# Values' product on array tiles of 64 rows by 32 columns instead of 64 by 64

## The chip, the cores and the metric

The kernel runs on one core of one Trainium2 chip. The time is that of the device for one execution, in microseconds (us); a smaller one is better. Before the change the median of three runs is 661.97 us, and they lie from 660.65 to 662.07. The engines are TensorE (PE in the profile, with its weight loads as PEld), VectorE (DVE), ScalarE (ACT), GpSimd (POOL) and SyncE (SP, which issues transfers).

## The reference

Eight batches go through windowed attention, then through a gated convolution, then through a gated block that mixes positions:

```python
scores = scale * np.matmul(q, k.transpose(0, 1, 3, 2))     # (8, 8, 576, 64) each
# heads 0-3: the last 32 positions; heads 4-7: every 4th of the last 128
scores = np.where(masks[None, :, :, :], scores, -1000000000.0)
scores = scores - np.max(scores, axis=-1, keepdims=True)
attn = np.exp(scores)
attn = attn / (np.sum(attn, axis=-1, keepdims=True) + 1e-09)
x = np.matmul(attn, v)                                      # heads side by side: (8, 576, 512)
gate = sigmoid(causal_conv5(x, conv_w))
x = gate * (x @ w_val) @ w_out
h = np.maximum(x @ w_in, 0.0)
u, v = h[..., :512], h[..., 512:]
v_n = (v - mean(v)) / np.sqrt(var(v) + 1e-06)
v_s = np.einsum('ts,bsd->btd', w_spatial, v_n) + b_spatial
out = (u * v_s) @ w_out2
```

## The kernel before

All work lies on one core, batch after batch. Each batch has an attention part, four pairs of heads (p = 0 to 3; the two heads of a pair lie in partitions 0 to 63 and 64 to 127), and a part of large products (`val`, `v`, `u`, `sp`, `out`) with 128 by 128 tiles of the array. The attention of a later batch is put in between the large products of an earlier one. The order is written out by hand: two tables, `EARLY` for the start and `EVERY` with a period for the rest, give each piece of work a due time; a queue sorted by these times emits the instructions, and each engine runs its own in that order.

For a pair of batches 2 to 7 (the third to the eighth) the attention does this. `a_scores` multiplies queries with keys: 36 products, each with 64 rows (the values of a head), 32 weight columns (32 queries) and 64 moving columns (64 keys), so tiles of 64 by 32 of the array. Mask, maximum, exponential and sum follow on other engines, then a transpose on VectorE and small transfers put the weights of the attention into `pt_later`. `a_pv` clears the border of its output tile and goes on in `pv_later`, which the change touches: the values' product. Its weights are the values `u` (64 keys by 64 value columns of one head), its moving operand is `pt_later` (64 keys by 96 queries). Five blocks `j` of 128 keys, two heads `h` and two halves `r` of a block (the last block has one half) give 18 products, written to the accumulator `o`: the head's 64 partitions, and a bank of the accumulator for each half `r`. Each is a product in 32-bit floats. After it, ScalarE and VectorE add the two halves into the input of the convolution (`xt`, or `tt` for the second four heads).

TensorE takes instructions in the written order. In most places of batches 3 on, the values' product of one pair is followed directly by the scores of a later pair (`qk_t`, `s_ps`), and then by the large products again. All instructions are emitted by one helper (line 635), so the rows of the profile have that one line, and groups are told apart by their tiles: `o_ps` is the accumulator of the values' product, `s_ps` that of the scores.

Of the kernel before, what the change touches and what calls it, by code (L numbers as in the profile page):

```python
# [25 lines left out]
QB = 32  # L26
# [647 lines left out]
def attention_gated_mlp_kernel(  # L674
# [29 lines left out]
    pt_later = pt.rearrange("p a b c q -> p (a b c q)")[:, 0:2 * NK * 96]  # L704
    pt_later = pt_later.rearrange("p (h j i q) -> p h j i q", h=2, j=NK, i=3)
# [26 lines left out]
    def matmul(o, a, r, start, stop):  # L732

        ten.matmul(o, a, r, start=start, stop=stop)
# [189 lines left out]
    def a_pv(b, p):  # L924
        if b == 0:
            xt = act.tile([128, 4 + S], F32, tag=f"xh{p}", name="xt")
            xh[b, p] = xt[:, 4:]
        else:
            xt = rot.tile([128, XW], F32, tag="xt", name="xt")
        gps.memset(xt[:, 0:4], 0.0)  # L930
        yield
        u = vv_t.pop((b, p))
        o = ps_o.tile([128, 1024], F32, tag="o", name="o_ps")
        if b >= 2:
            yield from pv_later(b, p, u, o, xt)
            return
        for j in range(NJ):
            c = 512 * (j // 3) + 96 * (j % 3)
            for h in range(2):
                r = slice(64 * h, 64 * h + 64)  # L940
                matmul(o[r, c:c + 96], u[:, j, r], pt[:, :, h, j], True, True)
        o = o.rearrange("p (a c) -> p a c", a=2)[:, :, 0:HS]
        if p < 2 and (b or p == 0):
            o_t[b, p] = o
        yield
        x_t[b, p] = xt
        if p < 2:
            sca.copy(out=xt[:, 4:4 + S].rearrange("p (a c) -> p a c", a=2), in_=o)
        else:
            sca.copy(  # L950
                out=xt[:, 4:4 + S].rearrange("p (i a r) -> p a r i", a=2, r=2),
                in_=o.rearrange("p a (r i) -> p a r i", r=2),
            )

    def pv_later(b, p, u, o, xt):


        for j in range(NK):
            for h in range(2):
                d = slice(64 * h, 64 * h + 64)  # L960
                for r in range(2 if j < NK - 1 else 1):
                    k = slice(64 * r, 64 * r + 64)
                    w = pt_later[k, h, j].rearrange("p i q -> p (i q)")
                    matmul(o[d, 512 * r + 96 * j:512 * r + 96 * j + 96], u[k, j, d], w, True, True)
        yield
        y = xt[:, 4:]
        if p >= 2:
            tt[b, p] = y = act.tile([128, S + 64], F32, tag=f"tt{p}", name="tt")
        gap = y[:, 96:96 + 512].rearrange("p (j c) -> p j c", c=128)[:, :, 0:QB]
        gps.memset(gap, 0.0)  # L970
        yield
        sca.copy(
            out=y[:, 0:640].rearrange("p (j c) -> p j c", c=128)[:, :, 0:96],
            in_=o[:, 0:480].rearrange("p (j c) -> p j c", c=96),
        )
        yield
        later = y[:, 64:64 + 512].rearrange("p (j c) -> p j c", c=128)[:, :, 0:96]
        vec.tensor_tensor(
            out=later, in0=o[:, 512:896].rearrange("p (j c) -> p j c", c=96), in1=later, op=ALU.add
        )  # L980
        if p >= 2:
            yield
            sca.copy(
                out=xt[:, 4:4 + S].rearrange("p (i g) -> p g i", g=4), in_=y[:, 0:S].rearrange("p (g i) -> p g i", g=4)
            )
        x_t[b, p] = xt
# [484 lines left out]
```

## Time and profile before

| | |
|---|---|
| median of 3 runs | 661.97 us (660.65 to 662.07) |
| span of the profiled execution | 659.2 us |
| TensorE busy | 638.3 us, 97% |
| VectorE busy | 455.7 us, 69% |
| GpSimd busy | 309.1 us, 47% |
| ScalarE busy | 305.2 us, 46% |
| granted TensorE clock, mean | 0.999 |

The span goes from the first to the last instruction that the profiler recorded; the timed runs hold something more than the span. Busy time is the union of an engine's instructions, and a product in 32-bit floats stands in it as two matmuls and two weight loads. A matmul's duration counts from its start to the end of what it writes, so matmuls that follow each other overlap in the records. A time line merges neighbours of one kind in a row with a count; asked for a short window, it shows the instructions that are in flight in the window, with the start of the earliest.

### The profile page before, as it was taken

The page shows a single profiled execution, that of the slowest core. Times are in us where ns is not written, and L with a number is a line of the kernel's source. Part 1 is how long each engine was busy: PE and PEld are TensorE (multiplying, and loading weights), DVE is VectorE, ACT ScalarE, POOL GpSimd, SP SyncE. Part 2 cuts the span into 40 slices and gives each one's busy share as a digit, 9 for nine tenths or more (in the row PEclk, how much of TensorE's full clock was granted, in tenths as well). Part 3 has the DMA queues.
Part 4 walks back from the last instruction along what each step waited for, and adds up shares of the span by engine and source line. Part 5 has one row for each costly group of instructions (what it writes and reads, how often), then busy time and mean ns, then how long its engine had stood idle before and what let it go on. Part 6 is the DMA issues. An engine that isn't in the chain of part 4 may idle for free.

```text
span 659.2 us, 17770 instructions
## 1 busy us (share of the span) xinstructions
PE 638.3 (97%) x7248; PEld 586.2 (89%) x7248; DVE 455.7 (69%) x789; ACT 305.2 (46%) x702; POOL 309.1 (47%) x378
## 2 busy tenths in 40 slices
PE   2899999999999999999999999999999999999998
PEld 2547789999899989999899989999899989999997
DVE  4999688997686677767666688767676688533410
ACT  4887666444443434344443435443443434442422
POOL 1114996746543374436634464426634464524430
PEclk9999999999999999999999999999999999999999
DMA  8981333353133332343123433343133411120002
GB/s 326 407 296 38 113 106 126 87 153 71 39 108 81 87 78 78 79 133 96 34 76 96 117 74 77 80 131 99 31 75 97 119 40 41 19 75 1 1 1 72
DMA packets 85605, 63.58 MB, mean 96 GB/s; under 512 B 64530, under 2 KB 74642, under 8 KB 85012
## 3 DMA queue, kind: packets, MB, share of 16 engines
q1 hardware_dynamic: 76308, 53.01, 28.5%
q10 hardware_dynamic: 9216, 9.44, 4.2%
q8 instruction: 57, 0.93, 0.6%
q14 instruction: 24, 0.20, 0.1%
HBM read 44.92 MB, written 9.44 MB: 82 GB/s over the span
## 4 chain that ended last, share of the span: by engine, by line
PE 82%; DVE 9%; DMA 3%; ACT 3%; POOL 2%; issue 1%; SPq 0%; DVEq 0%; POOLq 0%
PE sp_ps L635 17%; PE out_ps L635 15%; PE u_ps L635 14%; PE v_ps L635 14%; PE val_ps L635 14%; PE o_ps L635 4%; PE s_ps L635 3%; DVE tt L635 3%; DMA raw<-in_w_in 2%; DMA raw<-in_w_mid_t 1%; DVE wo_f L635 1%; DVE wiu_f L635 1%; POOL wsp_l L635 1%; ACT pt L635 1%; DVE v_t L635 1%
## 5 line engine op out<-in xcount | busy, mean ns | idle before, releaser
L635 DVE SCALAR_TENSOR_TENSOR tt<-xt,cw,tt 128x576 f32<-128x576 f32 x116 | 118.6, 1028 | 1.2
L635 PE MATMUL sp_ps<-wsp_h,vh 128*128 128x288 f32 x320 | 93.7, 297 | 0.0
L635 POOL TENSOR_TENSOR gl<-tt,gh 128x288 fp32r<-128x288 f32 x64 | 61.1, 963 | 49.6 <-ACT gh L635 45.9
L635 POOL TENSOR_TENSOR g2l<-ru,g2h 128x288 fp32r<-128x288 f32 x64 | 55.7, 877 | 53.8 <-ACT g2h L635 53.6
L635 PE MATMUL u_ps<-gh,w_h 128*128 128x288 f32 x256 | 76.3, 298 | 0.0
L635 PE MATMUL out_ps<-g2h,wout_h 128*128 128x288 f32 x256 | 76.2, 298 | 0.0
L635 PE MATMUL out_ps<-g2h,wout_l 128*128 128x288 f32 x256 | 75.4, 295 | 0.1
L635 PE MATMUL out_ps<-g2l,wout_h 128*128 128x288 f32 x256 | 75.4, 295 | 0.0
L635 PE MATMUL sp_ps<-wsp_l,vh 128*128 128x288 f32 x256 | 75.4, 294 | 0.0
L635 PE MATMUL u_ps<-gh,w_l 128*128 128x288 f32 x256 | 75.4, 294 | 0.0
L635 PE MATMUL u_ps<-gl,w_h 128*128 128x288 f32 x256 | 75.4, 294 | 0.0
L635 PE MATMUL sp_ps<-wsp_h,vl 128*128 128x288 f32 x256 | 75.4, 294 | 0.0
L635 PE MATMUL val_ps<-xh,wval_h 128*128 128x288 f32 x224 | 67.0, 299 | 0.0
L635 PE MATMUL val_ps<-xl,wval_h 128*128 128x288 f32 x224 | 66.2, 296 | 0.0
L635 PE MATMUL val_ps<-xh,wval_l 128*128 128x288 f32 x224 | 66.1, 295 | 0.0
L635 POOL TENSOR_TENSOR xl<-xt,xh 128x576 fp32r<-128x576 f32 x28 | 42.6, 1523 | 47.4 <-ACT xh L635 46.1
L635 POOL TENSOR_TENSOR vl<-v_t,vh 128x512 fp32r<-128x512 f32 x32 | 41.9, 1311 | 41.8 <-ACT vh L635 41.8
L635 PEld LDWEIGHTS sp_ps<-wsp_h,vh 128*128 128x128 f32 x320 | 60.0, 188 | 0.8
L635 POOL TENSOR_TENSOR e_t<-e_t,sm 128x576 f32<-128x576 f32 x31 | 38.1, 1229 | 47.8 <-DVE sm L635 22.7
L635 PE MATMUL v_ps<-w_h,gh 128*128 128x512 f32 x160 | 59.5, 396 | 0.6 <-DVE tt L635 0.6
L635 PE MATMUL v_ps<-w_l,gh 128*128 128x512 f32 x160 | 59.3, 395 | 0.0
L635 ACT CAST g2h<-ru 128x288 fp32r<-128x288 f32 x64 | 27.2, 431 | 64.7 <-DVE ru L635 64.5
(127 smaller groups left out, 1645.3 us busy)
## 6 DMA issues: line engine op xcount, KB each, us to landing
qk_t<-in_qk SPq DMA_DIRECT2D x30, 592.0 KB, 4.4
vv_t<-in_vv SPq DMA_DIRECT2D x30, 384.0 KB, 3.6
out<-ob ACTq DMA_DIRECT2D x64, 144.0 KB, 1.8
raw<-in_w_in SPq DMA_DIRECT2D x4, 1024.0 KB, 4.9
pt<-et SPq DMA_DIRECT2D x240, 16.0 KB, 1.9
pt<-et SPq DMA_DIRECT2D x144, 20.0 KB, 2.9
raw<-in_w_mid_t SPq DMA_DIRECT2D x2, 1024.0 KB, 12.5
raw<-in_w_val SPq DMA_DIRECT2D x2, 1024.0 KB, 12.7
```

Source lines behind the costliest of these rows:

```text
L635: ins = self._tc.keep_in_program_order(fn(*args, **kwargs))
```

## The change

The values' product of batches 2 to 7 takes 32 of a head's 64 value columns at a time. The loop over two heads becomes a loop over four column blocks `q` of 32 (`QB` is 32); the block decides which partitions of the accumulator are written and which columns of the values are the weights, and `q // 2` is the head. There are 36 products instead of 18, each on a tile of 64 rows by 32 columns. The moving operand, its 96 columns, the accumulator, its banks and the order of the other instructions are as before.

```diff
         for j in range(NK):
-            for h in range(2):
-                d = slice(64 * h, 64 * h + 64)
+            for q in range(4):
+                d = slice(QB * q, QB * q + QB)
                 for r in range(2 if j < NK - 1 else 1):
                     k = slice(64 * r, 64 * r + 64)
-                    w = pt_later[k, h, j].rearrange("p i q -> p (i q)")
+                    w = pt_later[k, q // 2, j].rearrange("p i q -> p (i q)")
                     matmul(o[d, 512 * r + 96 * j:512 * r + 96 * j + 96], u[k, j, d], w, True, True)
```

On TensorE, where a values' product stands ahead of scores, the written order before is this (out, then its operands, then partitions by columns of the output and the count):

```order
L635 MATMUL val_ps<-xh,wval_h 128x288
L635 MATMUL val_ps<-xl,wval_h 128x288
L635 MATMUL val_ps<-xh,wval_l 128x288
L635 MATMUL o_ps<-pt,vv_t 64x96 x18
L635 MATMUL s_ps<-qk_t 32x64 x36
```

At the same place after the change:

```order
L635 MATMUL val_ps<-xh,wval_h 128x288
L635 MATMUL val_ps<-xl,wval_h 128x288
L635 MATMUL val_ps<-xh,wval_l 128x288
L635 MATMUL o_ps<-pt,vv_t 32x96 x36
L635 MATMUL s_ps<-qk_t 32x64 x36
```

The 18 products have become 36 with half as many output partitions; nothing else has moved, here or on the other engines.

## Rows read from the trace of the kernel before

**Rows 1.** The profile's page: busy time of each engine, and the chain by engine.

```profile
PE 638.3 (97%) x7248; PEld 586.2 (89%) x7248; DVE 455.7 (69%) x789; ACT 305.2 (46%) x702; POOL 309.1 (47%) x378
...
PE 82%; DVE 9%; DMA 3%; ACT 3%; POOL 2%; issue 1%; SPq 0%; DVEq 0%; POOLq 0%
```

**Rows 2.** Stretch, length, then busy us of PE, PEld, DVE, ACT, POOL; granted clock.

```profile
302.07:376.44 74.37, 74.37 (x889) 70.41 (x889) 52.35 (x95) 31.84 (x62) 34.74 (x46) 1.00 0.33 87
...
450.80:525.17 74.37, 74.37 (x889) 70.40 (x889) 51.85 (x95) 31.71 (x62) 34.71 (x46) 1.00 0.34 87
```

**Rows 3.** Groups by form: tile rows*columns, moving shape, count | busy us, mean ns.

```profile
L635 PE MATMUL s_ps<-qk_t 64*32 64x64 f32 x2160 | 32.1, 230 | 10.6 <-DMA qk_t<-in_qk 8.7 <-DVE e_t L635 1.0 <-issue 0.8
L635 PE MATMUL o_ps<-pt,vv_t 64*64 64x96 f32 x864 | 25.6, 248 | 0.0
...
L635 PEld LDWEIGHTS s_ps<-qk_t 64*32 64x32 f32 x2160 | 27.0, 109 | 15.6 <-issue 7.9 <-DMA qk_t<-in_qk 4.8 <-DVE e_t L635 0.6
...
L635 PEld LDWEIGHTS o_ps<-pt,vv_t 64*64 64x64 f32 x864 | 21.1, 133 | 4.1 <-issue 3.8
```

**Rows 4.** Time line of TensorE around a block with scores: start us, us, form, count.

```profile
302.07 1.05 PE L635 MATMUL o_ps<-pt,vv_t 64*64 64x96 f32 x36
303.05 0.97 PE L635 MATMUL s_ps<-qk_t 64*32 64x64 f32 x72
303.95 0.40 PE L635 MATMUL val_ps<-xh,wval_h 128*128 128x288 f32 x1
```

**Rows 5.** Time line of TensorE around a block that stands alone.

```profile
565.45 1.05 PE L635 MATMUL o_ps<-pt,vv_t 64*64 64x96 f32 x36
566.43 0.40 PE L635 MATMUL sp_ps<-wsp_h,vh 128*128 128x288 f32 x1
```

**Rows 6.** Time line of TensorE around a block behind scores.

```profile
186.89 0.97 PE L635 MATMUL s_ps<-qk_t 64*32 64x64 f32 x72
187.79 1.15 PE L635 MATMUL o_ps<-pt,vv_t 64*64 64x96 f32 x36
188.88 0.40 PE L635 MATMUL sp_ps<-wsp_h,vh 128*128 128x288 f32 x1
```

**Rows 7.** Matmuls in flight at 302.50 and 302.75 us: first start, count.

```profile
302.29 0.43 PE L635 MATMUL o_ps<-pt,vv_t 64*64 64x96 f32 x12
...
302.53 0.43 PE L635 MATMUL o_ps<-pt,vv_t 64*64 64x96 f32 x12
```

**Rows 8.** The tiles' instructions: count, duration in ns (min/median/max), first and last start.

```profile
L635 PE MATMUL o_ps<-pt,vv_t x1008: 242/243/297, 27.2 to 583.1; 64*64 64x96 f32 x144, 128*64 128x96 f32 x24
...
L635 PE MATMUL s_ps<-qk_t x2160: 212/216/312, 4.8 to 550.0; 64*32 64x64 f32 x197
```

**Rows 9.** Windows 303.05 to 303.30, .33, .38; loads at 303.45, and 303.45 to 303.65.

```profile
302.86 0.26 PE L635 MATMUL o_ps<-pt,vv_t 64*64 64x96 f32 x2
303.05 0.45 PE L635 MATMUL s_ps<-qk_t 64*32 64x64 f32 x32
...
303.05 0.48 PE L635 MATMUL s_ps<-qk_t 64*32 64x64 f32 x33
...
303.05 0.54 PE L635 MATMUL s_ps<-qk_t 64*32 64x64 f32 x34
...
303.38 0.17 PEld L635 LDWEIGHTS s_ps<-qk_t 64*32 64x32 f32 x8
...
303.38 0.37 PEld L635 LDWEIGHTS s_ps<-qk_t 64*32 64x32 f32 x32
```

**Rows 10.** Time line of TensorE where transposes and scores of batch 0 meet.

```profile
17.07 0.31 PE L635 MATMUL s_ps<-qkv 64*32 64x64 f32 x1
17.16 0.33 PE L635 MATMUL t_ps<-ident_sb,e_t 64*32 64x64 f32 x4
17.18 0.31 PE L635 MATMUL s_ps<-qkv 64*32 64x64 f32 x1
```

## The prediction

> **What bounds the kernel now.** I read the totals first. TensorE is busy for 97% of the span and the next engine for 69% [rows 1]; the chain that ended last is 82% TensorE [rows 1]. Averages hide stages, so I then read the steady batches one by one: in each of three stretches of 74.37 us, of which the first and the last stand for all, TensorE is busy for all 74.37 us, at the full granted clock, while VectorE needs some 52 and GpSimd 35 [rows 2]. From batch 3 on, then, every nanosecond added to or taken from TensorE's stream moves the end by as much; a later or earlier end of one values' product changes nothing for the engines that read it, because TensorE waits for none of them there. So the sum is one over TensorE's stream alone.
>
> What do the two products weigh? The form with 64 by 64 tiles has 864 matmuls and 25.6 us, which is 24 blocks (six batches by four head pairs) of 36 matmuls; each written matmul is recorded as two, each with its own weight load, so a block is 18 products [rows 3]. The scores have 72 matmuls in a block, on tiles of 64 by 32 [rows 3, 4].
>
> How do the 24 blocks stand? In 15, scores follow directly: from the first values' matmul (302.07) to the first score (303.05) is 0.98, from there to the next work (303.95) 0.90, together 1.88 us [rows 4]. Seven stand alone among large matmuls (150.9, 170.5, 227.4, 267.3, 283.9, 565.5 and 582.3 us), each again 0.98 [rows 5]. In two, at 187.8 and 209.6 us, the scores come first; the first of the two stands for both [rows 6].
>
> **Inside a block.** A look at one instant gives the earliest matmul still in flight; the first and the last of four such looks, one step apart each, give starts at 302.29 and 302.53 with 12 in flight [rows 7]. Three steps in 0.24: the four tiles run side by side, each takes a new matmul every 0.08 us, and one lasts 0.243 [rows 7, 8]. The tiles on rows 0 to 63 have five key blocks of two matmuls, ten steps: about 0.83 us. The remainder of the 0.98 is the first weight load, some 0.05 (the longest matmul is 297 ns against a median of 243 [rows 8]), and the emptying before another shape begins: the last two matmuls start from 302.86, the first score at 303.05 [rows 4, 9].
>
> **What the change does to these.** A block now has 36 products, 72 matmuls, on eight tiles instead of 18 products on four. Each tile still sees five key blocks of two matmuls with 96 columns. The stream of the longest tile is thus unchanged at ten steps, 0.83 us, provided that eight tiles run as freely as four. The scores show that: eight tiles of exactly this shape start 32 matmuls in under 0.25 us [rows 9], which is four in each tile. The first load is of 32 columns instead of 64; a load of 64 has a mean of 133 ns and one of 32 of 109 [rows 3], so this saves about 0.02. Nothing else is issued: no DMA, wait or other engine's instruction is added.
>
> First price: the queue runs dry. In the scores, 32 matmuls, with their loads, start by 303.30, then by 303.33 only one matmul more, by 303.38 another [rows 9]. 32 matmuls and 32 loads are 64 instructions, or 16 products; then a place seems to come free only as an earlier matmul ends (the first started at 303.05 and lasts 0.24). After that, loads come at 24 in 0.20 us (32 less the 8 already in flight [rows 9]), 8.3 ns each, 16.7 ns for a product. The values' block of 18 products hardly passed 16; one of 36 does. By hand, from its first start: two matmuls on the first tile start at 0.03 and 0.11; the second ends at 0.35, and with about 0.03 until the place is used the 17th product's second matmul starts at 0.38. The 23rd, the last tile's third key block on rows 0 to 63, comes six products later, at 0.48 to 0.50. Its tile was free at 0.40. It is 0.10 late, and six steps follow on that tile, so a block that stands alone takes 1.08 instead of 0.98: seven times 0.10 is **+0.70 us**. No row shows it for 96 columns; the bounds are 0 (less the load's 0.02), if the queue refills in time, and 0.13, if the pace is 20 ns.
>
> Second, the gain: no change of shape before the scores. A trace of equal shapes exists at 17.07 us: scores on 64 by 32 start between transposes on 64 by 32, the next transposes at 17.16 and another score at 17.18, with no emptying [rows 10]. By that the scores start when the first tile has finished its ten steps, 0.03 + 0.83, at 0.86 instead of 0.98, whereas the late tile finishes at 0.99 and has only eight score steps to do. Then how long do the scores take? If at 16.7 ns for each of 36 products, 0.60, with 0.08 for the last second half and 0.14 for emptying 0.82. If as now, 0.90. They lose their burst of 16, for all 64 places are taken when they come, so I take the upper, 0.90. The pair is 0.86 + 0.90 = 1.76 against 1.88, a gain of 0.12; the other end is 1.68, a gain of 0.20. 15 times 0.12 is **-1.80 us**. For the two blocks behind scores a change of shape goes too; the one shown takes 1.09 us instead of 0.98 [rows 6], so something else delays its starts; I take 0.08 each, **-0.16**, between 0 and 0.20.
>
> **Sum.** +0.70 - 1.80 - 0.16 = -1.26 us. The profiled execution spans 659.2 us, so 657.9 after; the 2.8 us between that and the median of the timed runs, 661.97, stay, and the forecast is **660.7**. That is -0.19%; about 0.2% (1.3 us) is what a measurement here can tell from no change, so the likeliest case lies on that line.
>
> One rule speaks against this change. No gap between two starts in the scores comes near 25 ns on average: 32 start in under 0.25 us [rows 9], some 7 ns each. The Trainium skill, page "TensorE: Matmul & The Clock Gate", section "Wait — 56ns, not 53.3ns?", says that the distance from start to start never falls below about 25 ns, however small the matmul. By that floor 72 matmuls would take 1.8 us instead of some 0.9, an estimate of about 22 us more over 24 blocks. The trace contradicts the rule on separate tiles, and the measurement decides.
>
> **Rivals.** (A) *No run-dry at all:* the queue is refilled while the tiles step on, since eight tiles need 16 instructions in 0.083 us, 5.2 ns each, and the pace seen is 4.2. Then the pair is 1.68 and a lone block 0.02 shorter: -15 x 0.20 - 2 x 0.15 - 7 x 0.02 = -3.4 us, 658.5. Against it: the stall after the 32nd matmul is there in the scores. Chance 0.17.
>
> (B) *The scores pay it back:* the same 64 places now hold long matmuls (0.243 against 0.216 [rows 8]), so the scores come out slower than 0.90 by 0.07. The pair gains 0.05, the lone blocks lose 0.10: about 0, 662.0. Chance 0.10.
>
> (C) *The emptying stays, the run-dry comes:* if TensorE empties between two products for a reason other than shape (another accumulator, say), nothing is saved and 24 blocks take 0.10 more: +2.4 us, **664.4, slower**. The point from which it decides is the distance from the last values' matmul to the first score: at 0.17 or more there is no gain. Against it: transposes and scores, with different accumulators, mix at 17 us [rows 10]. Chance 0.05.
>
> (D) *Eight tiles run no faster than four,* because a half's four column blocks wait for one another with 96 columns: ten steps become twenty, 24 x 0.83 = +19.8 us, 681.8. The scores' 64 columns speak against it. This is also the outcome nearest to the page's floor of 25 ns. Chance 0.02.
>
> The forecast has 0.66, spread from -0.4 to -2.2 us by the bounds above. A little under half of it (0.30) lies past -1.3 us; with A that is 0.47 for faster. The rest, 0.36, with B is 0.46 for the same. C and D are 0.07 for slower. The range goes from A, 658.3, to 662.9, which holds B and a pair gain of nearly nothing with lone blocks at 0.13, but neither C nor D.
>
> **What would show it.** Lone blocks: 1.08 from the first values' matmul to the next work says run-dry; 0.96 says A. Pairs: 1.76 is the forecast, 1.68 is A, 1.83 B, 1.98 C, 2.7 D. A view of a pair should show scores starting while values' matmuls are still in flight and before the last of them has started; in the values' block, after 32 matmuls, a dent like that of the scores. The steady batch should be 74.37 less four times 0.12, near 73.9 us. The forecast is wrong if TensorE no longer fills a steady batch, if the form 64 by 32 shows matmuls of another length than 0.243, or if lone blocks and pairs both move in one direction.

## The result, and the profile after

The change makes the kernel slower: 665.62 us (median of 6 runs, 664.07 to 666.98) against 661.73 us of the kernel before on the same chip, a ratio of 1.0061 with an interval of 1.0051 to 1.0072. The forecast was 660.7 us, with a range up to 662.9. The profiled execution has 666.98 us and spans 665.2 us, 6.0 us more than before.

The page of the kernel after: busy us and instructions of each engine, and of part 3 one of the queues that bring in instructions (packets, MB, share).

```profile
PE 640.3 (96%) x8112; PEld 587.9 (88%) x8112; DVE 456.0 (69%) x789; ACT 305.2 (46%) x702; POOL 308.7 (46%) x378
...
q8 instruction: 64, 1.05, 0.7%
```

Against [rows 1] there are 864 more matmuls and 864 more weight loads, as the change says; the other engines do what they did. TensorE is busy for 2.0 us more, and the span is 6.0 longer, so most of the loss is time in which TensorE does nothing. The second line is new: its counterpart before is `q8 instruction: 57, 0.93, 0.6%`. 1.05 MB in 64 packets is 16 KB each. Seven packets more for 1,728 matmuls and loads more is about one for 256, so this queue is TensorE's.

Where does TensorE stand still? Its waits (what it waited for, us in total, times, longest):

```profile
PE s_ps L635 <- DMA qk_t<-in_qk: 8.8, 2, 4.5
PE s_ps L635 <- issue: 4.6, 5, 1.4
PE t_ps L635 <- POOL e_t L635: 3.0, 1, 3.0
PE o_ps L635 <- DMA pt<-et: 1.1, 1, 1.1
```

The first and third row are there before the change too. Of the second, one wait at 30 us is too (0.8 us then, 1.0 now); the other four are new: TensorE is in the middle of scores and has nothing to issue, and no other engine, semaphore or DMA of the program is named. The last is a wait for the small transfers that fill `pt_later`.

First a pair in which nothing goes wrong, TensorE's time line (start, us, form, count):

```profile
302.44 1.03 PE L635 MATMUL o_ps<-pt,vv_t 64*32 64x96 f32 x68
303.25 0.24 PE L635 MATMUL s_ps<-qk_t 64*32 64x64 f32 x1
303.26 0.26 PE L635 MATMUL o_ps<-pt,vv_t 64*32 64x96 f32 x2
303.29 0.24 PE L635 MATMUL s_ps<-qk_t 64*32 64x64 f32 x2
303.31 0.24 PE L635 MATMUL o_ps<-pt,vv_t 64*32 64x96 f32 x1
303.32 0.24 PE L635 MATMUL s_ps<-qk_t 64*32 64x64 f32 x2
303.34 0.24 PE L635 MATMUL o_ps<-pt,vv_t 64*32 64x96 f32 x1
303.35 0.95 PE L635 MATMUL s_ps<-qk_t 64*32 64x64 f32 x67
304.23 0.40 PE L635 MATMUL val_ps<-xh,wval_h 128*128 128x288 f32 x1
```

The seam is as forecast: scores start before the last values' matmuls have started, 0.82 us after the block's first (forecast 0.86, before 0.98 [rows 4]). The whole pair takes 1.79 us. Now the pair at 361.18:

```profile
361.18 1.03 PE L635 MATMUL o_ps<-pt,vv_t 64*32 64x96 f32 x68
...
362.09 0.81 PE L635 MATMUL s_ps<-qk_t 64*32 64x64 f32 x56
364.35 0.33 PE L635 MATMUL s_ps<-qk_t 64*32 64x64 f32 x11 [1.45 <-issue]
364.61 0.40 PE L635 MATMUL out_ps<-g2h,wout_h 128*128 128x288 f32 x1
```

The same course, but eleven matmuls short of the end TensorE idles for 1.45 us, and the pair takes 3.43. What comes in meanwhile? The transfers between 361 and 363 us, the queue of instructions (packets, MB, share of 16 engines):

```profile
q8 instruction: 1, 0.02, 5.2%
```

One packet of instructions, and its share says that it took 0.052 x 16 x 2 us = 1.66 us. The trace has it from 361.18 to 362.84; TensorE goes on at 364.34. The other three look alike, and so does a fifth stop at 327.7 us, just behind its pair, where large products still in flight cover most of it: the packet's transfer begins at 325.66, 342.76, 379.52 and 403.28 us, and TensorE goes on at 328.10, 345.13, 381.90 and 405.71, 2.4 us later each time.

That the stops belong to packets shows in their places. What TensorE had begun by the end of each stop (stretch, length, then busy us and, in brackets, count of matmuls and of weight loads):

```profile
0.00:328.05 328.05, 311.28 (x4140) 273.93 (x4140) 257.53 (x427) 171.87 (x437) 166.50 (x197) 1.00 0.41 126
0.00:345.10 345.10, 327.90 (x4392) 290.22 (x4393) 269.69 (x449) 179.14 (x452) 173.74 (x206) 1.00 0.40 124
0.00:364.30 364.30, 345.66 (x4645) 307.57 (x4645) 281.63 (x468) 187.27 (x467) 180.55 (x215) 1.00 0.40 123
0.00:381.88 381.88, 362.13 (x4898) 323.62 (x4898) 292.56 (x488) 193.85 (x480) 187.84 (x225) 1.00 0.40 122
0.00:405.69 405.69, 385.27 (x5150) 343.89 (x5150) 310.19 (x523) 203.95 (x499) 201.55 (x243) 1.00 0.39 118
```

Matmuls and loads together: 8280, 8785, 9290, 9796, 10300, so 504 to 506 apart. The trace also records 207 semaphore instructions on TensorE and one drain at the very start, which these rows leave out; with them the stops stand after 8385, 8897, 9409, 9921 and 10433 instructions, exactly 512 apart each time, two packets of 256.

The wait at 30 us lies on the same grid. TensorE's time line there in the kernel before:

```profile
28.59 0.70 PE L635 MATMUL s_ps<-qk_t 64*32 64x64 f32 x40
30.09 0.41 PE L635 MATMUL s_ps<-qk_t 64*32 64x64 f32 x11 [0.81 <-issue]
```

It stands after 961 instructions, 29 packets of 256 ahead of the 8385, and a packet's transfer begins at 27.56 us, 2.5 us before TensorE goes on. All twelve kernels of this document wait at that count, 0.4 to 1.7 us, whichever instruction stands there. So the kernel before already had one such stop, in its start: it is the 0.8 of `issue` in [rows 3].

**The sum of the profiled execution.** Five stops: 0.2 + 0.7 + 1.6 + 1.3 + 0.9 = +4.7 us (each pair's time less 1.79; for the first, behind its pair, the gap between two starts of large products less the usual 0.13). The wait for small transfers at 455 us: that pair takes 3.66, +1.9. Fifteen pairs at 1.793 instead of 1.879: -1.3. Seven lone blocks at 1.075 instead of 0.979: +0.7. Two blocks behind scores: +0.4. Scores that stand alone: +0.1. The start of the kernel, which the change does not touch, ran 0.45 shorter. Together +6.0. Leaving out the wait and the start, the sum is +4.6, and the medians differ by 3.9. This execution is the slowest of the six; the others have no profile, so whether they had the wait, and how long their stops were, is not shown.

### The profile page after: what moved, and what is told of

It reads as the page before. It is cut to its first block, busy times and chain, and to the rows that moved or that the text cites. A ratio compares the mean times of both kernels' runs of the same rounds, so it can differ in the third digit from the quotient of the medians.

```text
span 665.2 us, 19498 instructions
## 1 busy us (share of the span) xinstructions
PE 640.3 (96%) x8112; PEld 587.9 (88%) x8112; DVE 456.0 (69%) x789; ACT 305.2 (46%) x702; POOL 308.7 (46%) x378
## 3 DMA queue, kind: packets, MB, share of 16 engines
q8 instruction: 64, 1.05, 0.7%
## 4 chain that ended last, share of the span: by engine, by line
PE 79%; DVE 7%; DMA 4%; SPq 3%; ACT 2%; POOL 2%; issue 2%; DVEq 0%; POOLq 0%
PE sp_ps L635 17%; PE u_ps L635 14%; PE out_ps L635 14%; PE v_ps L635 14%; PE val_ps L635 12%; PE o_ps L635 4%; SPq L635 3%; PE s_ps L635 3%; DVE tt L635 2%; DMA raw<-in_w_in 2%; DMA qk_t<-in_qk 1%; DMA raw<-in_w_mid_t 1%; DVE wo_f L635 1%; DVE wiu_f L635 1%; POOL wsp_l L635 1%
```

## The experiments

Two theories. F, as the expectations call it: TensorE is stopped by the supply of its instructions. A pair of 288 matmuls and loads in 1.8 us uses up a packet of 256 faster than the next one comes, and whether it stops depends on where the pair lies against the packets' borders. Its rival: the tile shape itself, or its weight loads, is what holds up the scores. Then the same pairs stop wherever the packets' borders lie, and none stops without the new shape.

**Moving the borders.** Products that nobody uses, at the kernel's start, shift all that follows against the packets' borders, four TensorE instructions each; n was 24 and 40 on the changed kernel, and 40 on the kernel before as a control.

```diff
+    pad_ps = ps_o.tile([128, 1024], F32, tag="o", name="pad_ps")
+    flat = pt.rearrange("p a b c q -> p (a b c q)")
+    for i in range(n):
+        r, d = slice(64 * (i % 2), 64 * (i % 2) + 64), slice(64 * (i // 2 % 2), 64 * (i // 2 % 2) + 64)
+        matmul(pad_ps[d, 512 * (i % 2):512 * (i % 2) + 64], flat[r, 0:64], flat[r, 64:128], True, True)
```

> The changed kernel with 24 products on zeros added ahead of the first batch, while TensorE still waits for its first load; each is two matmuls and two weight loads, so all later TensorE instructions stand 96 places further on. Nothing else differs, and the products' output is not read. Theory F (fetch): TensorE's instructions come in blocks of 16 KB, 256 instructions; the changed kernel's five stops, at 328, 345, 363, 381 and 405 us, all lie where a block ends, because a values' product with scores eats 288 instructions in 1.8 us, faster than a block arrives. With the blocks' borders moved by 96 nearly no pair stands badly: stops of 0.4 to 1 us in sum instead of 4.9, so about 662 us (661.5 to 662.5) against 665.6 of the changed kernel. Theory M (matter of the tiles: array, banks or memory ports hold the eight tiles up, or other transfers collide): places in the instruction stream don't matter, 665 to 666 us.

Measured 661.82 us, a ratio of 1.0009 (0.9995 to 1.0022), and not one stop inside a pair. The whole loss is gone, with the change in place and 24 useless products more. A shape that holds up the scores can't explain that.

> As the one before, but with 40 products added, a move by 160 instructions, to places where more pairs stand badly. Theory F: stops of 4 to 6 us in sum, at other places than in the changed kernel, each where a block of 256 ends, so 665 to 667.5 us, 3 to 5 us slower than with 24 products although only 16 idle products differ. Theory M: the same time as with 24, 665 to 666 us, with the stops in the same pairs as in the changed kernel.

Measured 668.06 us, 1.0096 (1.0083 to 1.0109), above what was expected. Five stops, 4.4 us together (counted as above), but from 479 us on and at other pairs. Its waits for nothing that the profile shows (the first row holds three of the stops, the second the one at 479 us), then TensorE's counts by the end of the first two stops:

```profile
PE s_ps L635 <- issue: 2.6, 3, 1.2
...
PE u_ps L635 <- issue: 0.6, 1, 0.6
```

```profile
0.00:479.90 479.90, 461.21 (x6288) 417.22 (x6288) 363.80 (x620) 235.49 (x561) 236.91 (x288) 0.99 0.38 114
0.00:496.70 496.70, 477.77 (x6540) 433.42 (x6541) 375.24 (x640) 242.45 (x576) 243.18 (x296) 0.99 0.38 112
```

12576 and 13081 matmuls and loads; with the semaphore instructions 12737 and 13249. From the 8385 of the kernel after that is 17 times 256: the same borders, other pairs. About 3 us more were lost ahead of 170 us, as in the control that follows; that is why the time lies above the range.

> The kernel before with the same 40 products added. A pair has 216 instructions there and the borders' place should not matter: theories F and M both say 661.7 us (661.0 to 662.4), no stop. If the added products themselves cost something at the start, it is seen here: over 662.5 us.

A miss: 664.2 us, 1.0033 (1.0021 to 1.0045), where no change was expected; the cost at the start, which the expectation names as the other possibility, is what came. From 200 us on no stop lies at a packet's border. A memset on GpSimd starts 3.1 us later than before (173.12 against 170.06 us), and TensorE's stream is already 3.1 us late at 45 us. In that start TensorE waits 1.5 us, from 27.7 us on, and this wait does lie at a packet's border: it is the one after 961 instructions, with 0.8 us in the kernel before. Besides, TensorE runs at half the full granted clock for 3.4 us, from 37.9 us on (in the run above for 10.2 us, from 10.2 us on). How the 3.1 us divide among these and the products' own time is not shown. From 173 us to the end it takes 490.6 us against 489.1, and 1.4 of the difference is a wait for `pt<-et` at 528 us. So idle work at the start is not free, and after_pad40 has its five stops in addition to it.

**Pairs alone, lone blocks alone.** A condition on batch and pair chooses the tile's width:

```diff
-            for h in range(2):
-                d = slice(64 * h, 64 * h + 64)
+            w_ = QB if (3, 1) <= (b, p) <= (7, 1) and (b, p) not in ((3, 2), (3, 3)) else 64
+            for q in range(128 // w_):
+                d = slice(w_ * q, w_ * q + w_)
...
-                    w = pt_later[k, h, j].rearrange("p i q -> p (i q)")
+                    w = pt_later[k, q * w_ // 64, j].rearrange("p i q -> p (i q)")
```

This is `pairs`, the fifteen pairs alone. `pairs_one`, with `(b, p) == (2, 0) or` ahead of the condition, adds one lone block, 36 products for 18, so 72 TensorE instructions more ahead of the pairs; `pairs_pad16` has the 16 useless products, 64 instructions, instead; `lone` has the condition turned round.

> The change in the 15 blocks that scores follow alone, with nothing added. It differs from the one before by a single lone block of 36 products, at 150 us. Theory F: the first pairs of the steady part stand badly, stops of some 0.9 to 1.5 us each near 304, 327 and 344 us and none behind 385 us, 2 to 4.7 us in sum, where a block of 256 instructions ends; time 662.5 to 665 us, slower than before. Theory M: as the one before within 0.2 us.

> The change in the 15 blocks that scores follow and in the very first of the lone ones (150 us); the other eight keep 64 by 64. No product is added: the 72 more instructions of that first block move the later pairs against the borders of the 256-instruction blocks. Theory F: no stop; 15 times -0.09 and +0.10 make -1.25 us, so 660.5 us (660.0 to 661.2), the fastest of all. Theory M, or a wrong idea of where the borders are: stops as in the changed kernel, 664 us or more.

`pairs`: 665.18 us, 1.0063 (1.0045 to 1.0081), 0.2 above what F expected. `pairs_one`: 661.32 us, 0.9997 (0.9985 to 1.0010), 0.1 above. The kernel with one more block of the new shape is 3.9 us faster. Their waits for nothing shown, and for the small transfers, first of `pairs`:

```profile
PE s_ps L635 <- issue: 3.7, 4, 1.2
```

then of `pairs_one`:

```profile
PE o_ps L635 <- DMA pt<-et: 1.3, 2, 1.0
...
PE s_ps L635 <- issue: 0.9, 1, 0.9
```

`pairs` has five stops, 4.7 us together, the upper end of what F expected (its row holds three of them and one at 30.8 us; two, at 305.0 and 327.4 us, stand just behind their pairs), after 7361, 7873, 8385, 8897 and 9409 instructions; 512 apart again, and the last three are places of the kernel after as well. `pairs_one` has none inside a pair (the 0.9 is the wait at 30 us that the kernel before has too). In the profiled execution (662.02 us) the two waits for `pt<-et`, at 450 and 525 us, make their pairs 1.1 and 1.2 us longer; that such waits are why the median misses the forecast of 660.5 is tried out below.

> The change in the 15 blocks alone that scores follow; the other nine keep tiles of 64 by 64; 16 products on zeros added at the start (64 instructions). Theory F: by the places of the pairs no block border falls badly; the changed kernel's pairs without a stop last 1.79 instead of 1.88 us, so 15 times 0.086 is 1.3 us less than before: 660.4 us (659.9 to 661.0). Theory M: pairs are what stops, so some 5 us more than before, 666 us.

661.0 us, 0.9984 (0.9975 to 0.9994), the upper end of what was expected, and no stop in a pair; the first pair comes 1.2 us later than before, and one wait for `pt<-et` of half a microsecond stands at 451 us.

> The change in the nine other blocks alone (seven lone ones, two behind scores); the 15 before scores keep 64 by 64. Theory F: no stop at a block's end, since 216 instructions of a pair are too few and lone blocks are short; each lone block 1.07 instead of 0.98 us, with starts that falter after the first 32 matmuls; about 0.9 us more than before, 662.5 us in one look (661.5 to 663.5). If the pause after 32 matmuls is not from the queue of 64, the block shows an even pace.

661.66 us in one execution, inside what was expected, no stop in a block. A lone block takes 1.074 to 1.076 us, and the blocks behind scores lose 0.12 and about 0.2.

**Many instructions of the old shape.** The kernel before, with each score product of batches 2 to 7 written twice, so that a pair has 360 instructions and the values' tiles stay 64 by 64:

```diff
-                matmul(s[o:o + QB, cols], q, t[r, keys], True, True)
+                for _ in range(2 if b >= 2 else 1):
+                    matmul(s[o:o + QB, cols], q, t[r, keys], True, True)
```

> The kernel before, tiles of the values' product 64 by 64, with every score product of batches 2 to 7 issued twice in a row (the second writes the same numbers). A pair then has 360 instructions in some 2.6 us. Theory F: stops without any tile of the new shape in the values' product, each at the end of a block of 256 instructions, ten or more of them, 0.3 to 1.5 us each. Besides, 24 score blocks take some 0.6 to 0.8 us more, 14 to 19 us. Theory M: no stop, only the 14 to 19 us.

693.24 us in one execution. The 14 to 19 us expected for the doubled scores are a miss: a pair that doesn't stop takes 2.93 us instead of 1.88, so the 24 doubled blocks cost 1.05 us each, about 25 us, whatever the stops add. Its waits for nothing shown (the first row is four stops and the wait at 30 us, the others are one stop each), then TensorE's counts at the end of two stops:

```profile
PE s_ps L635 <- issue: 4.0, 5, 1.0
...
PE sp_ps L635 <- issue: 0.6, 1, 0.6
...
PE out_ps L635 <- issue: 0.3, 1, 0.3
```

```profile
0.00:422.30 422.30, 401.45 (x5789) 359.88 (x5790) 309.99 (x526) 204.24 (x500) 201.68 (x244) 1.00 0.38 114
0.00:478.00 478.00, 456.23 (x6675) 413.42 (x6676) 343.50 (x583) 226.08 (x542) 221.41 (x270) 1.00 0.38 112
```

Stops without the new shape: six from 200 us on, 0.5 to 1.2 us each, 6.0 together (counted as above): four in pairs, one (281 us) behind scores that stand alone, one (218 us) behind a values' product that follows scores. With the semaphore instructions the two shown stand after 11713 and 13505, again whole packets of 256 from the 8385 of the kernel after (13 and 20). So it is the count of instructions that stops TensorE, not the shape. There were fewer than the ten or more expected, because the expectation did not yet know the rule that follows.

**Which pairs stop.** The runs together give it. In the four kernels that stop from 200 us on, each such stop lies a whole number of packets from every other one. So each pair has a place against the borders: how many instructions of its packet lie ahead of its first one.

| kernel | instructions in a pair | place of its pairs, in order | stops |
|---|---|---|---|
| after | 288 | 176, 201, then 217, 228, 247, 245, 5, then 16 to 92 | at the five in the middle |
| pairs | 288 | 72, then 209, 225, 236, 255, 253, then 13 to 100 | at the five in the middle |
| after_pad40 | 288 | 80 to 195, then 209, 220, 239, 237, 253 | at the last five |
| after_pad24 | 288 | 16 to 189 | none |
| pairs_one, one_qk | 288 | 144, then 25 to 173 | none |
| pairs_pad16 | 288 | 136, then 17 to 164 | none |
| before | 216 | all over, also 223, 235 and 247 | none |
| before_twice | 360 | 213, 206, 194 and 200, between others from 14 to 130 | at these four |

A pair of 288 stops at places 209 to 5, all fifteen of them, and at no place from 13 to 201. From 224 on a whole packet lies inside the pair; from 209 to 220, and at 5, all but 4 to 15 of its instructions do. In the 360 of the last kernel the four pairs that stop are those that hold a whole packet. 216 instructions can't hold one, wherever they lie. The time says the same: the packet's transfer begins when some 250 instructions are left (192 to 285 in the five stops), and it takes 2.4 us (once 3.2) until TensorE can use it. In a pair of the changed kernel 250 instructions take 1.79 x 250/288 = 1.55 us, so 0.85 us are missing; before, 216 took 1.88 us, and the 34 around them, 17 large matmuls 0.133 us apart, 2.3: 4.1 us, more than enough. One block shows that time decides, and not the place alone: in before_twice at 191 us, scores ahead of values, 360 instructions hold a whole packet and don't stop; that packet's transfer begins 288 instructions ahead of the border, and TensorE takes 2.64 us to get there. And why five in a row? From pair to pair the kernel after has 523 instructions on average, two packets and 11: the place moves slowly, and once in the window, pair after pair falls into it.

**A version that beats both.** `pairs_one` has its places outside the window, and keeps the gain of the pairs; what its profile shows as lost are the waits for `pt<-et`. Those transfers are queued on SyncE, the first four and the last twelve with the load `qk_t` between them. `one_qk` is `pairs_one` with the load's due time, `load_qk` 3, moved back by 7.39 us; `before_qk` has that alone.

```diff
-    ("load_qk", 3): (211.61,),
+    ("load_qk", 3): (219.00,),
```

> The change in the 15 blocks before scores and in the first lone one (as in the earlier run of that kind, which had no stop at a block's end but waited 1.9 us in two batches for the small transfers of the attention's weights), and the load of the last pair's queries and keys moved behind those transfers in SyncE's queue. If those waits come from the queue, which then ends 0.5 us sooner, they are gone and the -1.25 us of the sum is left: 660.2 us, 0.2% less than before (659.8 to 660.9). If they come from slower landing alone: 661.3 as in the earlier run.

> The kernel before with that load moved alone. Its profile shows no wait for these transfers, so nothing should change: 661.5 us (661.0 to 662.0). If its timed runs often held such a wait, it gets faster by up to 0.7 us.

`one_qk`: 659.78 us, 0.9973 (0.9961 to 0.9984), faster than both kernels; no stop in a pair and no such wait. One of its steady batches (columns as in [rows 2]):

```profile
449.64:523.65 74.01, 74.01 (x1033) 70.51 (x1033) 52.26 (x95) 31.95 (x62) 34.72 (x46) 1.00 0.34 88
```

74.01 us against 74.37 before. `before_qk`: 660.96 us, 0.9989 (0.9977 to 1.0001): no difference that this shows. Of the 1.85 us that `one_qk` is faster, 0.67 are between the two kernels with the old tiles, and 1.18 between the two with the moved load; fifteen pairs at -0.086 and one lone block at +0.10 make -1.19. Whether the changed tiles make the wait for `pt<-et` more frequent is not settled: before_pad40, with the old tiles, had it too.

## Why the prediction was wrong

**The step that failed** is the sentence "Nothing else is issued: no DMA, wait or other engine's instruction is added". The 1,728 matmuls and loads themselves are added to what must be brought in, seven packets more. The prediction took its pace, 4.2 to 8.3 ns an instruction, from bursts of 32 to 64 and set it for 288 in a row; that a packet of instructions takes 2.4 us to come, and is asked for only about a packet ahead, it had not read anywhere, though one row had a sign of it, the 0.8 us of `issue` in [rows 3]. No rival had it either: C and D were slower for other reasons, and neither came. Worth +4.7 us in the profiled execution, and all of the measured loss, since the two kernels that only move the borders (after_pad24) or leave them harmless (pairs_one) are within 0.1% of the kernel before.

The Trainium skill has a sentence on this, page "Runtime: NRT & Kernel Launch", section "Instruction fetch mechanics": each engine's instructions are refilled in blocks of 16 KiB, 256 instructions, the next while the current one runs, and crossing a border is mostly hidden. The trace agrees with the block (64 packets of 16 KB, stops on a grid of exactly 256) and, for the kernel before, with "hidden": 57 packets, the one stop of 0.8 us at 30 us, and none in a steady batch. It does not agree for the kernel after, with 0.2 to 1.6 us at five borders.

**The gain of a pair** had the right mechanism and the wrong size: 0.086 us instead of 0.12, so -1.29 instead of -1.80. The scores start earlier than forecast, 0.82 us against 0.86, but then take 0.975 to the next work instead of 0.90: half of rival B is true. The steady batch without stops shows it (the last of the kernel after, columns as in [rows 2]):

```profile
480.15:554.15 74.01, 74.01 (x1033) 70.45 (x1033) 52.31 (x96) 31.77 (x62) 35.12 (x47) 1.00 0.32 79
```

74.37 less four times 0.09; forecast was 73.9. In the first steady batch of the kernel after, which has stops, TensorE is idle for 1.9 us:

```profile
302.44:379.08 76.64, 74.70 (x1033) 70.58 (x1032) 52.23 (x95) 31.75 (x62) 34.95 (x46) 1.00 0.33 85
```

**Lone blocks** were right: 1.08 forecast, 1.075 measured, here the one at 571 us in TensorE's time line, then the reason: weight loads begun within 0.24 and within 0.36 us of its start, and matmuls within the same.

```profile
571.24 1.15 PE L635 MATMUL o_ps<-pt,vv_t 64*32 64x96 f32 x72
572.32 0.40 PE L635 MATMUL sp_ps<-wsp_h,vh 128*128 128x288 f32 x1
```

```profile
571.24 0.35 PEld L635 LDWEIGHTS o_ps<-pt,vv_t 64*32 64x32 f32 x32 [0.16 <-issue]
...
571.24 0.46 PEld L635 LDWEIGHTS o_ps<-pt,vv_t 64*32 64x32 f32 x34 [0.16 <-issue]
...
571.24 0.48 PE L635 MATMUL o_ps<-pt,vv_t 64*32 64x96 f32 x24
...
571.24 0.60 PE L635 MATMUL o_ps<-pt,vv_t 64*32 64x96 f32 x33
```

32 loads begin within 0.24 us, only two more in the next 0.12: the dent after 32 loads and matmuls that was forecast. That a queue of 64 places makes it is argued from these counts, not shown.

**Blocks behind scores** had the wrong sign: a gain of 0.08 was taken, they lose 0.11 and 0.25. The first shows that a change of shape was not what it cost:

```profile
186.73 0.97 PE L635 MATMUL s_ps<-qk_t 64*32 64x64 f32 x72
187.61 1.29 PE L635 MATMUL o_ps<-pt,vv_t 64*32 64x96 f32 x72
188.83 0.40 PE L635 MATMUL sp_ps<-wsp_h,vh 128*128 128x288 f32 x1
```

The values start 0.88 us after the scores, 0.02 earlier than in [rows 6], and then take 1.22 instead of 1.09, a little more than the 0.10 that a lone block loses. Why these blocks are longer than lone ones at either shape stays open.

Without stops and waits the tile's own effect is -1.3 + 0.7 + 0.4 = -0.25 us where -1.26 was forecast: next to nothing. `after_pad24`, at 1.0009, is the run for it; its first changed block comes 0.65 us later than in the kernel before, so it can't tell the -0.25 from nothing.

## What to carry to other kernels

Splitting work over more and smaller array tiles buys overlap with instructions, and instructions have to be brought in: count TensorE's matmuls, loads and semaphores in the densest stretch, and where some 256 of them run in less than about 2.4 us, look for stops that come and go with where the stretch lies in the stream. A time that moves by 0.6% because something early was made a few dozen instructions longer is a sign of it; shift the stream by 64 to 96 instructions as a test before judging such a change. In the profile such a stop is idle time with `issue` as its reason in the middle of a run of equal matmuls, while a packet of TensorE's instructions is under way. Take the new shape only where it removes work from TensorE's stream (here the pairs, not the lone blocks).

## What the runs showed of the hardware

- TensorE's instructions come in packets of 16 KB, 256 instructions each; the transfer takes 0.9 to 1.7 us in the five stops, TensorE goes on 1.4 to 1.6 us after its end, and the packet is on its way only some 250 instructions before it is needed; of the kernel's other packets none begins more than 297 ahead. Why it is not asked for earlier, and why one transfer took 1.66 us, is open.
- Matmuls on different tiles start out of the written order: at 303.25 us a score starts ahead of the last four values' matmuls, written before it.
- Forty small idle products in the first microseconds put TensorE's stream about 3 us back by 45 us. Half the full granted clock, for 3.4 and 10.2 us in two runs, and a longer stop at a packet's border, 1.5 and 1.7 instead of 0.8 us, lie in that stretch; how the 3 us divide is open.
